# Folding the inverse transform over d a second time: odd and even frequencies apart, 144 columns to a product

## The chip, the cores and the metric

The kernel runs on one core of one Trainium2 chip. The metric is the device time of one execution in microseconds (us), as the median of several. Engines are named as in the profile: PE (TensorE, matrix products), PEld (its weight loads), DVE (VectorE), ACT (ScalarE), POOL (GpSimd) and SP (SyncE, which issues nearly all DMAs).

## The reference

The input x has 2048 rows (s) of 576 numbers (d). Rows are normalised, and two branches are added to x:

```python
xn = _layernorm(x, axis=-1)
# A: a filter in the frequencies of s and d
X = jnp.fft.rfft2(xn, axes=(-2, -1)) * (w_r + 1j * w_i)      # 2048 x 289
a = jnp.fft.irfft2(X, s=(S, D), axes=(-2, -1))
# B: a gated layer, F = 4608
h = _sigmoid(xn @ w_gate) * (xn @ w_up)
return x + a + h @ w_down
```

Everything is float32. The change concerns branch A alone, above all the last of its transforms, the inverse over d.

## The kernel before, in words

Products in float32 are made of two parts with a short mantissa (type fp32r, "hi" and "lo"): each factor is split, and three products (hi times hi, lo times hi, hi times lo) replace one. PE does all of it.

**Branch B** fills most of the span. `unit` (L667 on) makes one block of 128 of the 4608 hidden places for 1024 rows, with seven products (`prod`, L636) of seven instructions each, 512 columns wide, into PSUM banks A, B and E. The hidden values go through w_down in `down` (tile `po`, L743) and, in the second half of the rows, in `seven` (tile `ps`, L834), 288 columns wide. DVE adds `po` and `ps` into the accumulator `acc` or the sums `qs` (L747, L844).

**Branch A** is spread between these products in the second half of the program. Its steps are generators; the main loop calls `aside` after each of a unit's seven products, which moves each active generator to its next `yield`. A table (`begin`, from U1, U2, U3 at L41) says at which of these calls a step starts: `phase1b` (16 steps, forward over d and the first half of s), `phase2` (16 steps, second half of s, the filter, and the first half of the way back), `phase3` (16 steps t, a new one every 4.5 calls: second half of the way back over s, then the inverse over d). So the place of each instruction in PE's order is set by these numbers. DVE and ACT take theirs in nearly the program's order, moved a little by a scheduler.

The transform over d is **folded once**. With d measured from the middle, 287.5, cosines are even and sines are odd in d. So the cosine part is computed for 288 places only, the sine part too, and the two halves of d are their difference and sum. `COLS` orders the columns of x, w_down and the output so that the lower half stands first and the upper half, mirrored, behind it. The 289 frequencies stand in the order KOF (L44): 1 to 256, then 0, then 257 to 288, and one empty place make NQ = 290.

**A step of `phase3`** loads 2 x 128 rows of the intermediate result (`u`, from `sc2`), the matrices `ai` of that step and, for the first eight t, the rows of the result so far (`fin`, from `spill`); for the other eight, `acc` itself is added to. Then:

- `uh`, `ul` (L559, L560): the split of u. Products into `py` (L565), 290 columns: frequencies stand in the columns.
- `y` (L567): frequencies 1 to 256 are copied out of `py`. The remainder, FR = 33 columns, is split into `rp` (hi, lo, hi: 99 columns).
- `pz` (L577, L580): transposes, after which frequencies stand in the rows, 128 to a block k. z3h and z3l (L208, L209) are their two parts, z3r (L585, on ACT, the last of the three) is the remainder.
- `pe` (L594): for the cosine part e = 0 and the sine part e = 1 apart, 2 blocks x 3 products with z3h and z3l, then one with z3r. The constants `di` are the moving side, 288 columns; the z tiles are the weights. That is 14 products.
- the close: ACT copies the sine part to `od` (L596); DVE does lower - od, lower + cosine, upper + od, upper + cosine (L598, L599, L600, L601, each 288 wide). For the first eight t a DMA then writes the rows to the output.

`ps`, `po`, `py`, `pz`, `pe` and the like share one PSUM pool of two buffers (`pair`, tag `pp`), taken in turn: a tile can be filled when the tile two before it has been read. `stage3` (L622) makes room for phase 3 and loads `di`, and `stage2` clears the last column of zh and zl, which phase 2 doesn't write.

Of the kernel before, what the change touches and what calls it, by code (L numbers as in the profile page):

```python
# [24 lines left out]
FR = HD + 1 - 2 * P  # L25
# [18 lines left out]
KOF = np.array(list(range(1, 257)) + [0] + list(range(257, 289)))  # L44
# [19 lines left out]
def _constants():  # L64
# [5 lines left out]
    for e, v in ((0, np.cos(ang)), (1, -np.sin(ang))):  # L70
        m = np.zeros((HD, NQ))
        m[:, :KD] = v
        m[:, KD - 1 if e == 0 else KT * P] = 0.0
# [32 lines left out]

    a = np.where((KOF == 0) | (KOF == HD), 1.0, 2.0)[:, None] / (D * S)
    co, si = a * np.cos(ang.T), a * np.sin(ang.T)
    co[KD - 1] = 0.0
    si[KT * P] = 0.0  # L110
    t = np.zeros((P, 2, 5, HD), np.float32)
    for e, m in ((0, co), (1, si)):
        hi, lo = _split(m)
        for part, w in ((0, hi), (1, lo)):
            t[:, e, 2 * part] = w[:P]
            t[:, e, 2 * part + 1] = w[P:2 * P]
        t[:3 * FR, e, 4] = np.concatenate([hi[2 * P:], hi[2 * P:], lo[2 * P:]])
    out["di"] = t.reshape(P, 10 * HD)
# [4 lines left out]
COLS = np.concatenate([np.arange(HD), np.arange(HD, D)[::-1]])  # L123
# [3 lines left out]
def _layout(x, w_r, w_i, w_gate, w_up, w_down):  # L127

    ks = np.concatenate([np.arange(KT * P), np.tile(np.arange(KT * P, HD), 4)])
    w = np.stack([w_gate[COLS], w_up[COLS]]).reshape(2, 2, HD, NF, P)[:, :, ks]  # L130
    w = w[[1, 1, 0, 0], [0, 1, 1, 0]].reshape(4, KT + 1, P, NF, P).transpose(3, 2, 0, 1, 4)
    v = np.stack([w_r, w_i])[:, :, KOF].reshape(2, N1, N2 // 2, 2, KD).transpose(2, 1, 0, 3, 4)
    v = np.broadcast_to(v[:, None], (N2 // 2, 2, N1, 2, 2, KD))
    x = x.reshape(S, D)[ROWS][:, COLS]
    xt = x.reshape(NT, P, 2, HD)[..., ks].reshape(NT, P, 2, KT + 1, P).transpose(0, 4, 2, 3, 1)
    xg = xt[TPP:].reshape(2, TPC, P, 2, KT + 1, P).transpose(0, 3, 2, 4, 1, 5).reshape(2, 2, P, (KT + 1) * CW)
    lay = {"x": x.reshape(NT, P, D), "xt": xt.reshape(NT, P, 2 * (KT + 1) * P), "xg": xg, "ri": v.reshape(N2 // 2, P, 4 * KD),
           "w": w.reshape(NF, P, 4 * (KT + 1) * P), "wd": w_down[:, COLS].reshape(NF, P, D)}
    return {k: np.ascontiguousarray(a) for k, a in lay.items()}
# [9 lines left out]
def spectral_glu_kernel(ctx: ExitStack, tc: tile.TileContext, x, xt, xg, ri, w_in, w_down, out):  # L149
# [353 lines left out]
    def phase2(i):  # L503
# [4 lines left out]
        w = pool.tile([P, 2, 2, KD], F32, tag="ri", name=f"ri{i}", bufs=2)  # L508
# [14 lines left out]
        sw = pool.tile([P, 2, KD], F32, tag="sw", name=f"sw{i}")  # L523
        nc.scalar.activation(sw[:N1], pb[N1:, :, :KD], AF.Copy, scale=-1.0)
        nc.scalar.activation(sw[N1:], pb[:N1, :, :KD], AF.Copy)
        z = pool.tile([P, 2, KD], F32, tag="z", name=f"z{i}")
        t2 = pool.tile([P, 2, KD], F32, tag="t2", name=f"t2{i}")
        nc.vector.tensor_tensor(z, wr, pb[:, :, :KD], op=OP.mult)
# [3 lines left out]
        split(zh[:, :, :KD], zl[:, :, :KD], z)  # L532
# [10 lines left out]
    def phase3(t):  # L543
        pool, di = R["pool"], R["di"]
# [43 lines left out]
        for e in range(2):  # L588
            steps = []
            for k in range(2):  # L590
                steps += [(zh[:, k, e, :], di[:, e, k, :]), (zl[:, k, e, :], di[:, e, k, :]), (zh[:, k, e, :], di[:, e, 2 + k, :])]
            steps.append((zr[:3 * FR, e, :], di[:3 * FR, e, 4, :]))
            for n, (l, r) in enumerate(steps):
                nc.tensor.matmul(pe[:, e, :HD], l, r, start=n == 0, stop=n == len(steps) - 1)  # L594
        od = pool.tile([P, HD], F32, tag="od", name=f"od{t}")
        nc.scalar.activation(od, pe[:, 1, :HD], AF.Copy)  # L596
        lo, up = a[:, :HD], a[:, HD:]
        nc.vector.tensor_tensor(lo, lo, od, op=OP.subtract)  # L598
        nc.vector.tensor_tensor(lo, lo, pe[:, 0, :HD], op=OP.add)  # L599
        nc.vector.tensor_tensor(up, up, od, op=OP.add)  # L600
        nc.vector.tensor_tensor(up, up, pe[:, 0, :HD], op=OP.add)  # L601
# [9 lines left out]
    def stage2():  # L611
        pool = room("2")
        R["bm"] = bm = pool.tile([P, 4, P], F32R, name="bmt")
        load_r(bm, con["bm"].rearrange("p (k m) -> p k m", k=4))
        zh = pool.tile([P, 2, NQ], F32R, name="zh")
        zl = pool.tile([P, 2, NQ], F32R, name="zl")
        for z in (zh, zl):
            nc.vector.memset(f32(z)[:, :, KD:], 0.0)
# [606 lines left out]
```

## Time and profile before

| | |
|---|---|
| median of 3 runs | 1419.71 us (1419.65 to 1420.62) |
| the profiled execution | 1421.62 us |
| its span, first to last instruction | 1419.8 us |
| PE busy | 1405.9 us, 99% of the span, 7883 products |
| PEld busy | 1235.9 us, 87% |
| DVE busy | 1112.5 us, 78% |
| ACT busy | 640.6 us, 45% |
| DMA | 343.10 MB, mean 242 GB/s |
| mean granted PE clock | 0.997 |

The profile is of one execution. A group's row names line, engine, operation, the tiles (out<-in), shapes and count; then its busy time and the mean length of one; then the engine's idle time in front of it and what ended it. Products on PE overlap: one is as long as from its start to the end of its result, so that the distance between starts, in the timeline, is what a product costs in a stream. PEld rows are the weight loads, one to each product. Line numbers are those of the kernel before.

### The profile page before, as it was taken

The page shows a single profiled execution, that of the slowest core. Times are in us where ns is not written, and L with a number is a line of the kernel's source. Part 1 is how long each engine was busy: PE and PEld are TensorE (multiplying, and loading weights), DVE is VectorE, ACT ScalarE, POOL GpSimd, SP SyncE. Part 2 cuts the span into 40 slices and gives each one's busy share as a digit, 9 for nine tenths or more (in the row PEclk, how much of TensorE's full clock was granted, in tenths as well). Part 3 has the DMA queues.
Part 4 walks back from the last instruction along what each step waited for, and adds up shares of the span by engine and source line. Part 5 has one row for each costly group of instructions (what it writes and reads, how often), then busy time and mean ns, then how long its engine had stood idle before and what let it go on. Part 6 is the DMA issues. An engine that isn't in the chain of part 4 may idle for free. (4 is left out here: it accounts for less than half of the span.)

```text
span 1419.8 us, 20725 instructions
## 1 busy us (share of the span) xinstructions
PE 1405.9 (99%) x7883; PEld 1235.9 (87%) x7883; DVE 1112.5 (78%) x1722; ACT 640.6 (45%) x1035; POOL 3.3 (0%) x5
## 2 busy tenths in 40 slices
PE   8999999999999999999999999999999999999998
PEld 6888888888888888888888888888888889999897
DVE  6988888888888888789466888877878877766784
ACT  5644444444444443444235444434545534434431
POOL 0000000000000000000000000000000000000000
PEclk9999999999999999999999999999999999999999
DMA  6498677777777776675767777778888787766643
GB/s 250 181 329 308 256 267 262 270 263 270 263 269 263 269 263 247 242 254 176 270 217 234 224 234 223 217 245 267 275 269 272 236 290 221 247 215 204 195 126 84
DMA packets 130899, 343.10 MB, mean 242 GB/s; under 512 B 12176, under 2 KB 51632, under 8 KB 125936
## 3 DMA queue, kind: packets, MB, share of 16 engines
q1 hardware_dynamic: 129872, 340.47, 71.0%
q8 instruction: 62, 1.02, 0.3%
q10 hardware_dynamic: 928, 1.31, 0.3%
q14 instruction: 37, 0.30, 0.1%
HBM read 205.60 MB, written 136.13 MB: 241 GB/s over the span
## 5 line engine op out<-in xcount | busy, mean ns | idle before, releaser
L636 PE MATMUL pB<-X,w 128*128 128x512 f32 x1484 | 379.9, 393 | 0.0
L636 PEld LDWEIGHTS pB<-X,w 128*128 128x128 f32 x1484 | 268.0, 188 | 49.6 <-ACT v L700 1.3
L636 PE MATMUL pE<-X,w 128*128 128x512 f32 x1064 | 271.8, 392 | 0.5 <-DVE y L701 0.5
L636 PE MATMUL pA<-X,w 128*128 128x512 f32 x1008 | 261.4, 395 | 1.2 <-DVE X L445 0.8
L636 PEld LDWEIGHTS pE<-X,w 128*128 128x128 f32 x1064 | 193.2, 188 | 35.4 <-DVE y L701 1.0
L636 PEld LDWEIGHTS pA<-X,w 128*128 128x128 f32 x1008 | 184.5, 190 | 35.4 <-DVE X L445 1.7
L743 PE MATMUL po<-wd,hh 128*128 128x288 f32 x1216 | 210.8, 295 | 0.0
L834 PEld LDWEIGHTS ps<-wf,hs 128*128 128x128 f32 x1260 | 188.9, 188 | 17.9 <-ACT qs L842 0.9
L834 PE MATMUL ps<-wf,hs 128*128 128x288 f32 x1260 | 202.0, 295 | 0.4 <-ACT qs L842 0.4
L743 PEld LDWEIGHTS po<-wd,hh 128*128 128x128 f32 x1216 | 184.2, 188 | 11.8 <-ACT hh L726 0.4
L747 DVE TENSOR_TENSOR acc<-acc,po 128x576 f32<-128x576 f32 x168 | 125.7, 749 | 67.3 <-PE po L743 66.8
L240 ACT ACTIVATE w<-raw 128x768 fp32r<-128x768 f32 (+1 forms) x106 | 100.8, 952 | 93.1 <-PE pE L636 36.5
L743 PE MATMUL po<-wd,hl 128*128 128x288 f32 x608 | 128.7, 293 | 0.0
L844 DVE TENSOR_TENSOR qs<-qs,ps 128x576 f32<-128x576 f32 x112 | 84.1, 751 | 28.4 <-PE ps L834 27.4
L743 PEld LDWEIGHTS po<-wd,hl 128*128 128x128 f32 x608 | 98.7, 189 | 0.0
L701 DVE TENSOR_TENSOR y<-v,pE 128x512 f32<-128x512 f32 x68 | 46.7, 686 | 52.2 <-ACT v L700 51.3
L844 DVE TENSOR_TENSOR acc<-acc,ps 128x576 f32<-128x576 f32 x90 | 67.5, 750 | 23.3 <-PE ps L834 22.6
L242 DVE TENSOR_TENSOR w<-raw,w 128x512 fp32r<-128x512 f32 (+1 forms) x106 | 81.8, 772 | 3.2 <-ACT w L240 2.9
L721 DVE TENSOR_TENSOR y<-y,g 128x1024 f32<-128x1024 f32 x67 | 81.9, 1222 | 3.1
L770 ACT ACTIVATE hs<-y 128x512 fp32r<-128x512 f32 x105 | 64.8, 628 | 38.2 <-DVE y L721 14.6
L704 ACT ACTIVATE g<-pB 128x512 f32<-128x512 f32 x68 | 40.7, 598 | 89.9 <-PE pB L636 89.9
L700 ACT ACTIVATE v<-pB 128x512 f32<-128x512 f32 x68 | 40.6, 598 | 71.0 <-PE pB L636 70.7
(175 smaller groups left out, 1609.0 us busy)
## 6 DMA issues: line engine op xcount, KB each, us to landing
w<-wsp SPq DMA_DIRECT2D x246, 320.0 KB, 3.5
wsp<-w SPq DMA_DIRECT2D x34, 2240.0 KB, 7.8
raw<-in_w SPq DMA_DIRECT2D x34, 768.0 KB, 9.7
wdsp<-wd SPq DMA_DIRECT2D x36, 576.0 KB, 4.6
wf<-tsp SPq DMA_DIRECT2D x60, 288.0 KB, 3.9
wf<-wdsp SPq DMA_DIRECT2D x45, 288.0 KB, 3.9
std<-in_wd SPq DMA_DIRECT2D x36, 288.0 KB, 5.5
ri<-in_ri SPq DMA_DIRECT2D x16, 578.0 KB, 5.3
```

What stands on the lines that cost most here:

```text
L240: placed(nc.scalar.activation(o[:, :, :3, :], src, AF.Copy))
L242: placed(nc.vector.tensor_tensor(o[:, :, 3:, :], src[:, :, :KT, :], f32(o[:, :, :KT, :]), op=OP.subtract))
L636: nc.tensor.matmul(bank, w[:, sw, :], X[:, x, sx, :], start=start and j == 0, stop=stop and j == len(STEPS) - 1, skip_group_check=skip)
L700: nc.scalar.activation(v[:, 1], bank["B"], AF.Copy)
L701: nc.vector.tensor_tensor(y[:, 1], v[:, 1], bank["E"], op=OP.add)
L704: nc.scalar.activation(g[:, 1], bank["B"], AF.Sigmoid)
L721: nc.vector.tensor_tensor(y, y, g, op=OP.mult)
L743: nc.tensor.matmul(pd[:, b, :HD], h[i], w[k][b], start=g == 0 and n == 0, stop=g == G - 1 and n == 2)
L747: nc.vector.tensor_tensor(a, a, pd[:, :, :HD], op=OP.add)
L770: nc.scalar.activation(hs[:, 0], src, AF.Copy)
L834: nc.tensor.matmul(pd[:, i, :HD], h[:, a, m], w[:, b], start=q == 0, stop=q == 2)
L844: nc.vector.tensor_tensor(o, o, pd[:, :, :HD], op=OP.add)
```

## The change

The inverse over d is folded a second time. Within half of d, 288 places from the middle out, a cosine of an even frequency is even about the quarter, and that of an odd frequency odd; for sines it is the other way. So each part needs 144 places only (HQ), one set for odd and one for even frequencies, and the four quarters of d come from their sums and differences.

- KOF puts the 144 odd frequencies first, then an empty place (PAD), then the 145 even ones. Blocks for the transposes are places 0 to 127 (odd only) and 162 to 289 (even only); the remainder is the 34 places between them, 16 odd, the empty one and 17 even.
- `di` now has, for each part e, block k and half (hi, lo), 144 columns. The remainder's constants stand in `dr` (tile `drt`), still 288 wide, with zeros in the quarter set that a row has no part in. They are loaded separately.
- In `pe` the product with the remainder comes first and opens the PSUM bank; the twelve others add to one half of it, 144 columns each.
- The close: `ev` takes cosine part + od and cosine part - od (two operations of 288); one of 576 adds the even set of both to all four quarters (the same 288 numbers to both halves of the row); two of 288 add and subtract the odd set.
- `COLS` orders columns by quarters. `cf`, `ri` and the layouts of x, made on the host, follow the new orders; the remainder in `rp` has 3 x 34 = 102 columns. In phase 2 all 290 columns are worked on in place of 289, and the two memsets are gone.

```diff
-KOF = np.array(list(range(1, 257)) + [0] + list(range(257, 289)))
+KOF = np.array(list(range(1, HD, 2)) + [0] + list(range(0, HD + 1, 2)))
...
-COLS = np.concatenate([np.arange(HD), np.arange(HD, D)[::-1]])
+COLS = np.concatenate([HD - 1 - QTR, HD + QTR, QTR, D - 1 - QTR])
...
     def phase3(t):
...
-        nc.scalar.activation(y, py[:, :, :2 * P], AF.Copy)
+        main = py[:, :, :2 * (P + FR)].rearrange("p a (b n) -> p a b n", b=2)[..., :P]
+        nc.scalar.activation(y.rearrange("p a (b n) -> p a b n", b=2), main, AF.Copy)
         rp = pool.tile([P, 2, 3, FR], F32R, tag="rp3", name=f"rp3{t}")
-        rem = py[:, :, 2 * P:KD]
+        rem = py[:, :, P:P + FR]
...
         for e in range(2):
-            steps = []
+            nc.tensor.matmul(pe[:, e, :HD], zr[:3 * FR, e, :], dr[:3 * FR, e, :], start=True, stop=False, skip_group_check=True)
             for k in range(2):
-                steps += [(zh[:, k, e, :], di[:, e, k, :]), (zl[:, k, e, :], di[:, e, k, :]), (zh[:, k, e, :], di[:, e, 2 + k, :])]
-            steps.append((zr[:3 * FR, e, :], di[:3 * FR, e, 4, :]))
-            for n, (l, r) in enumerate(steps):
-                nc.tensor.matmul(pe[:, e, :HD], l, r, start=n == 0, stop=n == len(steps) - 1)
+                o = pe[:, e, (k + 1 + e) % 2 * HQ:((k + 1 + e) % 2 + 1) * HQ]
+                for n, (l, i) in enumerate(((zh, 0), (zl, 0), (zh, 1))):
+                    nc.tensor.matmul(o, l[:, k, e, :], di[:, e, k, i, :], start=False, stop=n == 2, skip_group_check=True)
         od = pool.tile([P, HD], F32, tag="od", name=f"od{t}")
         nc.scalar.activation(od, pe[:, 1, :HD], AF.Copy)
-        lo, up = a[:, :HD], a[:, HD:]
-        nc.vector.tensor_tensor(lo, lo, od, op=OP.subtract)
-        nc.vector.tensor_tensor(lo, lo, pe[:, 0, :HD], op=OP.add)
-        nc.vector.tensor_tensor(up, up, od, op=OP.add)
-        nc.vector.tensor_tensor(up, up, pe[:, 0, :HD], op=OP.add)
+        V = pool.tile([P, 2, 2, HQ], F32, tag="ev", name=f"ev{t}")
+        for i, op in ((0, OP.add), (1, OP.subtract)):
+            nc.vector.tensor_tensor(V[:, i].rearrange("p a q -> p (a q)"), pe[:, 0, :HD], od, op=op)
+        w = a.rearrange("p (s v q) -> p s v q", s=2, v=2)
+        nc.vector.tensor_tensor(w, w, V[:, :, 0].unsqueeze(1).to_broadcast([P, 2, 2, HQ]), op=OP.add)
+        for i, op in ((0, OP.add), (1, OP.subtract)):
+            nc.vector.tensor_tensor(w[:, i], w[:, i], V[:, :, 1], op=op)
...
     def stage3():
         pool = room("3")
-        R["di"] = di = pool.tile([P, 2, 5, HD], F32R, name="dit")
-        load_r(di, con["di"].rearrange("p (e k n) -> p e k n", e=2, k=5))
+        R["di"] = di = pool.tile([P, 2, 2, 2, HQ], F32R, name="dit")
+        R["dr"] = dr = pool.tile([P, 2, HD], F32R, name="drt")
+        load_r(di, con["di"][:, :8 * HQ].rearrange("p (e k i q) -> p e k i q", e=2, k=2, i=2))
+        load_r(dr, con["di"][:, 8 * HQ:].rearrange("p (e n) -> p e n", e=2))
```

PE's order stays the same but for the products of `pe` themselves. Here is the first step of phase 3 on PE before, from the products of a unit in front of `pe` to those behind it (128x288 is the result, rows by columns; dit is `di`):

```order
L834 MATMUL ps_5_1_11030<-wf_5_10891,hs_5_10941 128x288 x6
L594 MATMUL pe_11040<-dit,z3h_11015 128x288
L594 MATMUL pe_11040<-dit,z3l_11016 128x288
L594 MATMUL pe_11040<-dit,z3h_11015 128x288 x2
L594 MATMUL pe_11040<-dit,z3l_11016 128x288
L594 MATMUL pe_11040<-dit,z3h_11015 128x288
L594 MATMUL pe_11040<-dit,z3r_11017 128x288
```

The same place now, the first seven of its 14 products:

```order
L846 MATMUL ps_5_1_11030<-wf_5_10891,hs_5_10941 128x288 x6
L600 MATMUL pe_11040<-drt,z3r_11017 128x288
L604 MATMUL pe_11040<-dit,z3h_11015 128x144
L604 MATMUL pe_11040<-dit,z3l_11016 128x144
L604 MATMUL pe_11040<-dit,z3h_11015 128x144 x2
L604 MATMUL pe_11040<-dit,z3l_11016 128x144
L604 MATMUL pe_11040<-dit,z3h_11015 128x144
```

Seven instructions stay seven, with seven weight loads; six have half the columns, and the one with z3r has moved to the front.

On DVE, the close of the first step before, with the operations around it:

```order
L701 TENSOR_TENSOR y_10900<-v_10899,pE_10903 128x512
L844 TENSOR_TENSOR qs<-qs,ps_5_1_11030 128x576
L598 TENSOR_TENSOR fin_10875<-fin_10875,od_11055 128x288
L600 TENSOR_TENSOR fin_10875<-fin_10875,od_11055 128x288
L599 TENSOR_TENSOR fin_10875<-fin_10875,pe_11040 128x288
L601 TENSOR_TENSOR fin_10875<-fin_10875,pe_11040 128x288
L844 TENSOR_TENSOR acc<-acc,ps_6_0_11070 128x2x288
```

And now:

```order
L713 TENSOR_TENSOR y_10900<-v_10899,pE_10903 128x512
L856 TENSOR_TENSOR qs<-qs,ps_5_1_11030 128x576
L609 TENSOR_TENSOR ev_11057<-pe_11040,od_11055 128x288 x2
L611 TENSOR_TENSOR fin_10875<-fin_10875,ev_11057 128x576
L613 TENSOR_TENSOR fin_10875<-fin_10875,ev_11057 128x288 x2
L856 TENSOR_TENSOR acc<-acc,ps_6_0_11072 128x2x288
```

Four operations have become five, the one of 576 between the pairs; only the first two read `pe`.

More of the change, by code (lines that the diff above doesn't have):

```diff
@@ L70, in _constants @@
     for e, v in ((0, np.cos(ang)), (1, -np.sin(ang))):
-        m = np.zeros((HD, NQ))
-        m[:, :KD] = v
-        m[:, KD - 1 if e == 0 else KT * P] = 0.0
+        m = np.where(FREQ, v, 0.0)
         hi, lo = _split(m)
@@ L104, in _constants @@
     out["bm"] = b.reshape(P, 4 * P)
[L107 to L112, printed above, removed]
-        hi, lo = _split(m)
[L114 to L118, printed above, removed]
+    a = np.where((KOF == 0) | (KOF == HD), 1.0, 2.0)[:, None] / (D * S) * FREQ[:, None]
+    ang = 2 * np.pi * KOF[:, None] * (QTR[None, :] + 0.5) / D
+    t = np.zeros((P, 2, 2, 2, HQ), np.float32)
+    r = np.zeros((P, 2, HD), np.float32)
+    for e, m in ((0, a * np.cos(ang)), (1, a * np.sin(ang))):
+        m[KOF == (HD, 0)[e]] = 0.0
+        hi, lo = _split(m)
+        for k, rows in enumerate((slice(0, P), slice(NQ - P, NQ))):
+            t[:, e, k, 0], t[:, e, k, 1] = hi[rows], lo[rows]
+        h, l = np.zeros((2, FR, HD), np.float32)
+        for s, v in ((h, hi), (l, lo)):
+            v = v[P:NQ - P]
+            o = ODD[P:NQ - P]
+            s[o, (1 - e) * HQ:(2 - e) * HQ] = v[o]
+            s[~o, e * HQ:(e + 1) * HQ] = v[~o]
+        r[:3 * FR, e] = np.concatenate([h, h, l])
+    out["di"] = np.concatenate([t.reshape(P, 8 * HQ), r.reshape(P, 2 * HD)], 1)
     out["id"] = np.eye(P, dtype=np.float32)
     return out
-COLS = np.concatenate([np.arange(HD), np.arange(HD, D)[::-1]])
+COLS = np.concatenate([HD - 1 - QTR, HD + QTR, QTR, D - 1 - QTR])
 ROWS = np.arange(S).reshape(N1, N2).T.ravel()
@@ L507, in phase2 @@
         nc.sync.dma_start(x2, sc1.rearrange("(p kl) n -> p kl n", kl=N2)[:, kl:kl + 2])
-        w = pool.tile([P, 2, 2, KD], F32, tag="ri", name=f"ri{i}", bufs=2)
+        w = pool.tile([P, 2, 2, NQ], F32, tag="ri", name=f"ri{i}", bufs=2)
         nc.sync.dma_start(w.rearrange("p a j n -> p (a j n)"), ri[i])
@@ L522, in phase2 @@
                 nc.tensor.matmul(pb[:, j, :NQ], bm[:, k, :], m[:, j, :], start=n == 0, stop=n == 2)
[L523 to L528, printed above, removed]
+        sw = pool.tile([P, 2, NQ], F32, tag="sw", name=f"sw{i}")
+        nc.scalar.activation(sw[:N1], pb[N1:, :, :NQ], AF.Copy, scale=-1.0)
+        nc.scalar.activation(sw[N1:], pb[:N1, :, :NQ], AF.Copy)
+        z = pool.tile([P, 2, NQ], F32, tag="z", name=f"z{i}")
+        t2 = pool.tile([P, 2, NQ], F32, tag="t2", name=f"t2{i}")
+        nc.vector.tensor_tensor(z, wr, pb[:, :, :NQ], op=OP.mult)
         nc.vector.tensor_tensor(t2, wi, sw, op=OP.mult)
@@ L543, in phase3 @@
     def phase3(t):
-        pool, di = R["pool"], R["di"]
+        pool, di, dr = R["pool"], R["di"], R["dr"]
         u = pool.tile([P, 2, NQ], F32, tag="u3", name=f"u3{t}", bufs=2)
```

23 lines of the change are left out of this document (14 added, 9 removed).

## The prediction

> **What bounds the kernel now.** I read the page first, then the busy time by stretches, the waits, and last the timeline around one step of the changed phase. On the page PE is busy for nearly the whole span:
>
> ```profile
> span 1419.8 us, 20725 instructions
> PE 1405.9 (99%) x7883; PEld 1235.9 (87%) x7883; DVE 1112.5 (78%) x1722; ACT 640.6 (45%) x1035; POOL 3.3 (0%) x5
> ```
>
> The changed phase, `phase3`, runs from about 1150 to 1394 us. Two stretches of the view by windows cover it (columns: window, its length, busy us and instructions of PE, PEld, DVE, ACT, POOL, granted clock, DMA share, GB/s):
>
> ```profile
> 1180.00:1300.00 120.00, 120.00 (x716) 108.39 (x715) 87.77 (x146) 51.43 (x108) 0.00 (x0) 1.00 0.72 227
> 1300.00:1420.00 120.00, 115.09 (x701) 104.29 (x699) 79.52 (x123) 39.76 (x82) 0.00 (x0) 1.00 0.48 140
> ```
>
> PE has no gap in the first and 4.9 us in the second, which also holds the tail; DVE is busy for 73% and 66%. The waits say the same from both sides (engine and line, what it waited for, total us, times, longest):
>
> ```profile
> PE pE L636 <- DVE y L701: 0.5, 1, 0.5
> PE ps L834 <- ACT qs L842: 0.4, 1, 0.4
> PE po L743 <- DVE acc L747: 0.3, 1, 0.3
> DVE acc L747 <- PE po L743: 66.8, 52, 5.4
> DVE qs L844 <- PE ps L834: 27.4, 36, 1.8
> DVE acc L844 <- PE ps L834: 22.6, 28, 2.1
> ```
>
> PE waits for DVE for tenths of a microsecond in the whole span; DVE waits for PE for over 100 us in these three rows alone. So here the end moves by what PE's own stream of products gains or loses, and other engines' work counts only once it makes PE wait.
>
> **What one step of `phase3` costs on PE.** The products of tile `pe`, by kind, with their counts over the 16 steps:
>
> ```profile
> L594 PE MATMUL pe<-dit,z3h x128: 292/296/403, 1174.3 to 1391.7; 128*128 128x288 f32 x128
> L594 PE MATMUL pe<-dit,z3l x64: 290/296/298, 1174.5 to 1391.6; 128*128 128x288 f32 x64
> L594 PE MATMUL pe<-dit,z3r x32: 297/298/302, 1175.1 to 1391.9; 99*128 99x288 f32 x32
> ```
>
> That is 14 a step. The 296 ns are start to end of one; products overlap, so what counts is the distance from start to start. The timeline of the first step gives it (start, length, engine, line):
>
> ```profile
> 1174.35 0.29 PE L594 MATMUL pe<-dit,z3h 128*128 128x288 f32 x1
> ...
> 1176.21 1.79 PE L636 MATMUL pB<-X,w 128*128 128x512 f32 x7
> ...
> 1177.83 0.96 PE L834 MATMUL ps<-wf,hs 128*128 128x288 f32 x6
> ```
>
> Fourteen products in 1176.21 - 1174.35 = 1.86 us: **132.9 ns** each with 288 columns. Seven with 512 columns in 1.62 us: 231.4 ns. So a column costs (231.4 - 132.9) / 224 = 0.44 ns and a product 6 ns besides.
>
> **The change, part by part.** It leaves 14 products a step: the two remainder products (z3r) keep 288 columns, the other 12 go to 144. That is 192 in all (128 + 64). If columns alone set the distance, 144 of them would take 6.3 + 144 x 0.44 = 69.6 ns. But the number of weight loads stays, one of 128 columns for each product, and a load has a floor of its own. No product in the kernel with full 4-byte weights and so few columns shows it directly; it shows where PE stood idle and two loads followed with nothing in front (PEld rows, two places):
>
> ```profile
> 1316.72 0.19 PEld L594 LDWEIGHTS pe<-dit,z3h 128*128 128x128 f32 x1 [0.33 <-ACT z3r L585]
> 1316.83 0.19 PEld L594 LDWEIGHTS pe<-dit,z3l 128*128 128x128 f32 x1
> ```
>
> ```profile
> 964.69 0.19 PEld L538 LDWEIGHTS pc<-zh,bmt 128*128 128x128 f32 x1 [0.20 <-ACT zh L208]
> 964.80 1.02 PEld L636 LDWEIGHTS pA<-X,w 128*128 128x128 f32 x5
> ```
>
> Both pairs are 0.11 us apart, though one load lasts 0.19. The transposes, with 128 columns on both sides, give the same in a stream:
>
> ```profile
> L577 PE MATMUL pz<-idf,y x64: 270/272/328, 1171.3 to 1386.6; 128*128 128x128 f32 x64
> ```
>
> ```profile
> 1386.29 0.60 PE L577 MATMUL pz<-idf,y 128*128 128x128 f32 x4
> ...
> 1386.65 0.39 PE L580 MATMUL pz<-idr,rp 128*99 128x128 f32 x2
> ...
> 1386.87 1.83 PE L636 MATMUL pE<-X,w 128*128 128x512 f32 x7
> ```
>
> Four in 0.60 us, the last 0.272 long: (0.60 - 0.272) / 3 = 109.3 ns, where their columns alone would need 6.3 + 56 = 63 ns. I take **109.3 ns** for a product of 144 columns: the columns fit under the load. The bounds are 69.6 ns (loads hidden after all) and 132.9 ns (no gain).
>
> The Trainium skill has a rule for each side. "TensorE: Matmul & The Clock Gate", section "LDWEIGHTS (loading the stationary operand)", gives the load as the weight's columns over 1.2, in ns: 107 for 128, with which the sum would be 192 x 26 = 5.0 us; the 0.11 us between loads agree. The same page's section "Back-to-back issue gap" gives about 81 ns per product in a stream of loads and products with 128 columns, and 131 with 512; between the two, 144 columns would come to some 83 ns, an estimate, and the sum to 9.6 us. The 231 ns measured here for 512 columns contradict it, and no run here shows it for a short product.
>
> The sum: 192 x (132.9 - 109.3) ns = **4.5 us less on PE**, 0.28 us in each of 16 steps, all of it on the path.
>
> *VectorE.* The four closing operations become five. One step as it is, with what follows:
>
> ```profile
> 1176.85 0.46 DVE L598 TENSOR_TENSOR fin<-fin,od 128x288 f32<-128x288 f32 x1 [1.12 <-ACT od L596]
> 1177.23 0.45 DVE L600 TENSOR_TENSOR fin<-fin,od 128x288 f32<-128x288 f32 x1
> 1177.60 0.44 DVE L599 TENSOR_TENSOR fin<-fin,pe 128x288 f32<-128x288 f32 x1
> 1177.96 0.45 DVE L601 TENSOR_TENSOR fin<-fin,pe 128x288 f32<-128x288 f32 x1
> ...
> 1178.83 0.75 DVE L844 TENSOR_TENSOR acc<-acc,ps 128x576 f32<-128x576 f32 x1 [0.42 <-PE ps L834]
> ...
> 1180.23 0.96 PE L834 MATMUL ps<-wf,hs 128*128 128x288 f32 x6
> ...
> 1181.02 0.29 PE L565 MATMUL py<-uh,ai 128*128 128x290 f32 x1
> ```
>
> ```profile
> L560 DVE TENSOR_TENSOR ul<-u,uh 128x580 fp32r<-128x580 f32 x16 | 12.1, 758 | 2.2 <-ACT uh L559 1.8 <-DMA w<-wsp 0.3
> ```
>
> Four operations of 288 stay, 0.37 us apart; one of 576 comes, near the 0.76 us of the row of 580. So DVE works 0.76 us longer a step, 12 us in all, in about 240 us with some 70 us of idle time in the two stretches above. What is queued behind it is the add of the next `ps`, and PE waits for that add only for its buffer. There are two buffers in the pool of `pe`, `ps`, `py`, `pz`, taken in turn. After L601 DVE stood idle for 0.42 us, so the add would end 0.34 us later, at 1179.9; its buffer is taken by `py` at 1181.02, 1.1 us on. The buffer of `pe` is taken at 1180.23, and its last reader is now the second operation, not the fourth: 0.74 us sooner. I cost this at nothing; without that cover it is up to 12 us.
>
> *The remainder product goes first,* and reads z3r, the last tile made. The row of 1316.72 shows that the first product of `pe` waited for z3r already: `pe` takes the buffer that z3r is read from. Nothing new to wait for: nothing.
>
> *Constants and stage 2.* `dit` shrinks from 1.47 to 0.88 MB and comes in two loads, one more on SP's queue behind which the weights `w` stand. These wait for PE themselves:
>
> ```profile
> SPq L287 <- PE pB L636: 154.6, 89, 4.7
> ```
>
> One issue takes about 0.4 us there, in a queue that stands still for PE: nothing, or 0.4 us once. `ri` grows by 0.3%, operations of 578 become 580, and two memsets of a few columns go. All off PE's path: nothing. A few DVE operations swap places in stage 2 and 3, which may move PE's short waits by some tenths either way.
>
> **Against which time.** The profiled execution took 1421.62 us, its span 1419.80; the change makes them about 1417.1 and 1415.3. The median of the runs is 1419.71, 1.9 below the profiled one; the same 4.5 us off it give **1415.2 us**.
>
> **The rivals.**
> *A (forecast): the load is the floor,* 109 ns, 1415.2 us. For it: both pairs of loads and the transposes. Chance 0.72.
> *B: loads overlap more deeply,* and products come at between 70 and 100 ns. At 70 the gain is 192 x 63.3 = 12.2 us, 1407.5 us. For it speaks only that PEld rows last 0.19 us yet overlap; against it, the 0.11 us. The page's back-to-back figure lies inside it. Chance 0.07.
> *C: short products in this 4-byte type pass their columns more than once.* Narrower than 288 the trace has none but the transposes, and the two of L580 at 0.22 / 2 = 0.11 us each speak against it only if a transpose runs as an ordinary product does. The place is the 192 products; the turning point is 132.9 ns. Two passes give 6.3 + 127 = 133 ns, no change, 1419.7 us (chance 0.04). Four give 259.5 ns: 192 x 126.6 = 24.3 us more, **1444.0 us**, slower (chance 0.08).
> *D: DVE becomes late.* If all of its 12 us reach PE, 1419.7 - 4.5 + 12.1 = 1427.3 us. It decides from where the added 0.76 us a step exceed the slack, which is 0.42 us of idle time and then 1.1 us up to `py`. Against it: that slack, and the idle time. Chance 0.04; that part of it eats the gain down to under 2.8 us, 0.05.
>
> **How the numbers follow.** A measurement of this kernel can tell about 0.2%, 2.8 us, from no change. Faster by more: A and B less a little of A that ends just short, 0.76. Within: two passes, part of D and that remainder, 0.12. Slower: four passes and all of D, 0.12. The range takes in both bounds of the unknown distance, 1407 (69.6 ns) to 1420 (132.9 ns), and leaves out 0.12.
>
> **What would show it.** Right: the distance between the products of `pe` is 0.109 us, a step takes 2 x 0.133 + 12 x 0.109 = 1.57 us in place of 1.86, PEld rows of `pe` stand 0.11 us apart, and PE's idle time in phase 3 is as before. A step of 1.1 us shows B, of 1.86 or 3.4 us C. D would show as PE rows waiting for `acc`, `qs` or `y` on DVE, and as more PE idle time. It is wrong if the step's 14 products don't come closer together, or if the 0.28 us a step are given back at the next buffer.

## The result, and the profile after

| | before | changed |
|---|---|---|
| median | 1419.94 us (21 runs, 1419.20 to 1421.65) | 1417.93 us (21 runs, 1417.26 to 1419.47) |
| ratio, 95% interval | | 0.9986 (0.9980 to 0.9992) |
| profiled execution: span | 1419.8 us | 1415.8 us |
| from the first product of `pe` to the last of `po` | 240.8 us | 238.7 us |

The change saves 2.0 us, 0.14%. The forecast was 4.5.

The span isn't the number to read. The two executions differ by 2.0 us when phase 3 begins; in the thirteen profiles of this study phase 3 begins anywhere from 1172.1 to 1174.7 us, with the wide products and with the narrow ones alike. The difference is made at the very start: the 401st product of PE starts at 83.3 to 86.1 us, and from there to the first product of `pe` all thirteen profiles take 1088.6 to 1089.0 us. It goes with the granted clock of the first 60 us, here before and then changed (view by windows, columns as in the prediction; the clock is the third figure from the end):

```profile
0.00:60.00 60.00, 52.88 (x254) 41.02 (x255) 46.51 (x122) 37.97 (x80) 3.29 (x5) 0.94 0.53 196
```

```profile
0.00:60.00 60.00, 52.15 (x262) 40.09 (x263) 48.17 (x125) 39.68 (x83) 3.29 (x5) 1.00 0.56 204
```

The seven profiles in which phase 3 begins later than 1173 us are the seven with a mean clock of 0.997 over the span. The medians show it too: over the comparison sets of the experiments the kernel before took 1421.09 us at 0.997 (median of 31 runs) and 1419.85 at 0.998 (31). So the mechanism is read from phase 3, from the start of the first product of `pe` to that of the last of `po`, and the verdict from the ratios. That stretch went from 240.8 to 238.7 us, 2.1 less. For the changed kernel its ends stand in these two rows (line, engine, operation, count: shortest/median/longest ns, first to last start):

```profile
L600 PE MATMUL pe<-drt,z3r x32: 292/339/403, 1172.3 to 1387.0; 102*128 102x288 f32 x32
L755 PE MATMUL po<-wb,hp x192: 289/295/398, 1361.1 to 1411.0; 128*128 128x288 f32 x192
```

The 14 products of the first step in the timeline of the changed kernel (start, length, engine, line):

```profile
1172.31 0.30 PE L600 MATMUL pe<-drt,z3r 102*128 102x288 f32 x1
1172.45 0.23 PE L604 MATMUL pe<-dit,z3h 128*128 128x144 f32 x1
1172.52 0.27 PE L604 MATMUL pe<-dit,z3l 128*128 128x144 f32 x1
1172.63 0.39 PE L604 MATMUL pe<-dit,z3h 128*128 128x144 f32 x2
1172.85 0.28 PE L604 MATMUL pe<-dit,z3l 128*128 128x144 f32 x1
...
1173.88 1.83 PE L648 MATMUL pB<-X,w 128*128 128x512 f32 x7
```

A step takes 1173.88 - 1172.31 = 1.57 us where it took 1.86. The distance is 0.11 us between the short products, except from the first one behind a product of 288 columns to the next, where a load has already gone ahead (1172.45 to 1172.52, 0.07 us, which is what the prediction worked out for the columns alone). The loads stand as far apart as the products:

```profile
1172.45 0.19 PEld L604 LDWEIGHTS pe<-dit,z3l 128*128 128x128 f32 x1
1172.56 0.30 PEld L604 LDWEIGHTS pe<-dit,z3h 128*128 128x128 f32 x2
```

So the gain came as worked out, 0.29 us in this step, and part of it went elsewhere. The waits of PE from 1150 us on name where. Before there was one, `po` behind DVE at the very end; now:

```profile
PE pB L648 <- ACT pB L699: 0.5, 1, 0.5
PE py L575 <- DVE acc L856: 0.4, 1, 0.4
PE po L755 <- DVE acc L759: 0.3, 1, 0.3
PE py L575 <- issue: 0.2, 1, 0.2
```

Laying the starts of the products of both traces side by side (their order on PE differs only within `pe` and in stage 6, where one product of `pE` has moved ahead of five of `py`, at no cost) gives four places at which the distance to the next product has grown. Stage t reaches from the `pe` of step t, counted from 0, to that of the next step. The places are stage 4, where `py` starts 0.53 us later than it could (1234.87); stage 7, `ps` 0.11 us (1274.93); stage 10, `py` 0.41 us (1319.64); stage 13, `pB` 0.62 us (1359.37). Behind each stall the second product stands 0.08 to 0.11 us further off as well. In sum 2.0 us.

The place in stage 4, on DVE and on PE. Before:

```profile
1232.30 1.28 DVE L771 TENSOR_TENSOR hs<-y,hs 128x512 fp32r<-128x512 f32 x2
1233.61 0.46 DVE L598 TENSOR_TENSOR fin<-fin,od 128x288 f32<-128x288 f32 x1
...
1235.08 0.68 DVE L808 TENSOR_TENSOR y<-y,y 128x512 f32<-128x512 f32 x1
1235.68 0.75 DVE L844 TENSOR_TENSOR acc<-acc,ps 128x576 f32<-128x576 f32 x1
...
1237.78 0.29 PE L565 MATMUL py<-uh,ai 128*128 128x290 f32 x1
```

Changed:

```profile
1229.16 1.28 DVE L783 TENSOR_TENSOR hs<-y,hs 128x512 fp32r<-128x512 f32 x2
1230.36 1.41 DVE L820 TENSOR_TENSOR y<-y,y 128x512 f32<-128x512 f32 x2
1231.69 0.81 DVE L609 TENSOR_TENSOR ev<-pe,od 128x288 f32<-128x288 f32 x2
1232.53 0.76 DVE L611 TENSOR_TENSOR fin<-fin,ev 128x576 f32<-128x576 f32 x1
1233.33 0.83 DVE L613 TENSOR_TENSOR fin<-fin,ev 128x288 f32<-128x288 f32 x2
1234.07 1.41 DVE L856 TENSOR_TENSOR acc<-acc,ps 128x576 f32<-128x576 f32 x2
```

```profile
1233.55 0.96 PE L846 MATMUL ps<-wf,hs 128*128 128x288 f32 x6
1234.87 0.40 PE L575 MATMUL py<-uh,ai 128*128 128x290 f32 x1 [0.36 <-DVE acc L856]
```

`py` takes the buffer that the first of the two adds to `acc` reads. Before, that add ended at 1236.43 and `py` came at 1237.78: 1.35 us of slack. Measured from the start of the two `hs`, the add begins 3.38 us later before and 4.91 now. The close is 0.91 us longer (1233.61 to 1235.08, now 1231.69 to 1234.07), and **two operations `y` have moved ahead of it** (sums of hidden values, from which the factor `hs` of a later product `ps` is made), of which one stood ahead of the add already: some 0.6 us more. And PE could be at `py` 5.18 us after that start (six `ps` take 0.79 us) in place of 5.48, which is the step's own gain. 1.35 - 1.53 - 0.30 = -0.48 us, against 0.53 that `py` lost. None of the three alone is enough. By the same sum the close and the order together would exceed the slack by 0.2 us, and either one together with the earlier PE would not (the runs below with the old close, and those with the order held, have no wait here).

In stages 7 and 10 `y` operations have moved ahead of the close too, and in stage 13 two more copies on ACT ahead of the one that PE waits for. Before, and now:

```profile
1360.97 0.63 ACT L770 ACTIVATE hp<-y 128x512 fp32r<-128x512 f32 x1 [0.40 <-DVE y L721]
1361.79 0.58 ACT L687 ACTIVATE pB<-pA 128x512 f32<-128x512 f32 x1 [0.18 <-PE pA L636]
1362.28 1.14 ACT L770 ACTIVATE hp<-y 128x512 fp32r<-128x512 f32 x2
```

```profile
1357.68 1.14 ACT L782 ACTIVATE hp<-y 128x512 fp32r<-128x512 f32 x2
1358.73 0.59 ACT L699 ACTIVATE pB<-pA 128x512 f32<-128x512 f32 x1
```

### The profile page after: what moved, and what is told of

The parts are those of the page before. It is cut to its first block, busy times and chain, and to the rows that moved or that the text cites. A ratio compares the mean times of both kernels' runs of the same rounds, so it can differ in the third digit from the quotient of the medians.

```text
span 1415.8 us, 20731 instructions
## 1 busy us (share of the span) xinstructions
PE 1400.5 (99%) x7883; PEld 1228.9 (87%) x7883; DVE 1123.7 (79%) x1736; ACT 640.3 (45%) x1035; POOL 3.3 (0%) x5
```

## The experiments

Four theories were set against each other. **L**: the close, longer by one DVE operation, makes PE wait. **O**: the order does it; with shorter products the scheduler, which works from its own estimates, puts other DVE and ACT work ahead of the close. **P**: the earlier PE runs into work that ends when it did before, whatever the order. **E**: something else, away from these places. All results (ratio to the kernel before, run beside it; "phase 3" is the stretch defined above in the one profile of each kernel, 240.8 us before):

| run | products, close, order | median us | ratio (95%) | phase 3 |
|---|---|---|---|---|
| changed | 144, new, by the scheduler | 1417.93 | 0.9986 (0.9980 to 0.9992) | 238.7 |
| e1_old_close | 144, old, by the scheduler | 1417.88 | 0.9983 (0.9974 to 0.9992) | 238.9 |
| e2_wide | 288, new, by the scheduler | 1420.74 | 1.0001 (0.9993 to 1.0010) | 240.6 |
| e3_pool | 144, new with one operation on POOL | 1421.41 | 1.0002 (0.9994 to 1.0011) | 240.9 |
| e4_pin | 144, new, ACT's copies kept in order | 1417.86 | 0.9981 (0.9972 to 0.9990) | 238.2 |
| e5_old_held | 144, old, close ahead of `y` | 1416.84 | 0.9979 (0.9970 to 0.9988) | 237.3 |
| e6_held_last | 144, new, close ahead of `y` | 1417.33 | 0.9980 (0.9971 to 0.9989) | 237.4 |
| e7_held_first | 144, new, its first half ahead of `y` | 1417.34 | 0.9978 (0.9969 to 0.9987) | 237.1 |
| e8_72 | 72, new, by the scheduler | 1415.39 (one run) | | 236.7 |
| e9_wide_late | 288, new, `y` ahead of the close | 1421.11 | 1.0003 (0.9994 to 1.0012) | 240.6 |
| e10_one_held | 144, new, close ahead of one `y` | 1416.82 | 0.9976 (0.9967 to 0.9985) | 237.3 |
| e11_wide_exact | 288, new, stage 4 as in the changed | 1419.98 | 1.0001 (0.9992 to 1.0010) | 240.5 |

**The old close.** Four DVE operations again, with the products of the change; the sums of the odd and even parts over the quarters are left out of the computation.

```diff
-        for i, op in ((0, OP.add), (1, OP.subtract)):
-            nc.vector.tensor_tensor(V[:, i].rearrange("p a q -> p (a q)"), pe[:, 0, :HD], od, op=op)
...
+        nc.vector.tensor_tensor(lo, lo, od, op=OP.subtract)
+        nc.vector.tensor_tensor(lo, lo, pe[:, 0, :HD], op=OP.add)
+        nc.vector.tensor_tensor(up, up, od, op=OP.add)
+        nc.vector.tensor_tensor(up, up, pe[:, 0, :HD], op=OP.add)
```

> The changed kernel with the close of the kernel before: four operations of 288 on DVE, no operation of 576. It leaves out the sums over the odd and even sets, so the columns of branch A are wrong; PE's products are those of the change. In the changed kernel's trace PE waits at four places of phase 3 which were free before, about 2.2 us: three of them behind DVE (near 1234, 1275 and 1319 us), one behind ACT (1358.5 us), where ACT now copies two hp tiles ahead of pB<-pA. Theory L (DVE's longer close makes PE late): the three places behind DVE go, the one on ACT stays, since ACT's order there is still the changed one: 1419.9 - 4.6 + 0.7 = 1416.0 us, ratio to before 0.997. Rival O (only the new order on ACT and DVE costs, not the added operation): mostly as the changed kernel, 1417 to 1418 us, ratio 0.9986. Rival P (narrow products cost PE something later, whatever DVE does): 1417.9 us, with the waits in other places.

1417.88 us: nothing was won by the shorter close, and L as a single cause falls. The wait of stage 4 is gone, though both `y` still stand ahead of the close there, as the sum above would have it (0.91 us of it was the close), but those of stages 10 and 13 stand, and that of stage 7 has grown. The timeline of this kernel there, DVE and PE:

```profile
1274.17 0.69 DVE L818 TENSOR_TENSOR y<-y,y 128x512 f32<-128x512 f32 x1
1274.78 0.45 DVE L608 TENSOR_TENSOR fin<-fin,od 128x288 f32<-128x288 f32 x1
...
1275.88 0.45 DVE L611 TENSOR_TENSOR fin<-fin,pe 128x288 f32<-128x288 f32 x1
```

```profile
1276.43 1.06 PE L844 MATMUL ps<-wf,hs 128*128 128x288 f32 x6 [0.68 <-ACT v L704]
```

The row names ACT, but the product starts 0.10 us after the fourth operation of the close has ended, which is the last to read `pe` and frees the buffer. With the new close only the first two read `pe`, and the wait is 0.11 us. So the new close wins 0.7 us here, about the 0.6 that it costs in stage 4.

**Products of 288 columns with zeros**, the new close.

```diff
-    t = np.zeros((P, 2, 2, 2, HQ), np.float32)
+    t = np.zeros((P, 2, 2, 2, HD), np.float32)
...
-                o = pe[:, e, (k + 1 + e) % 2 * HQ:((k + 1 + e) % 2 + 1) * HQ]
+                o = pe[:, e, :HD]
```

> The changed kernel, but each of the twelve products of pe has 288 columns again, with zeros in the quarter set that it has no part in: PE's cost of before, DVE's close of the change. The result is the reference's. ACT's order at t = 13 is that of before here. Theory L: PE gives DVE 0.29 us more a step, so that the waits behind DVE are fewer than in the changed kernel but some are left: 0.5 to 1.5 us over before, 1420.4 to 1421.4 us, ratio 1.0004 to 1.001. Rival O: with other orders on DVE and ACT, 1420 to 1421 us. Rival P: 1419.9 us, no waits that before doesn't have. Rival E (something else in the change, say the constants or stage 2, gives or costs): clearly off this, under 1419 or over 1422 us.

1420.74 us, no change, and phase 3 within 0.2 us of before with none of the four waits. The longer close, the new constants, the new order of columns and the remainder product in front cost nothing that phase 3 shows; the forecast's zeros hold, as long as the products stay wide.

**The operation of 576 on POOL.**

```diff
-        nc.vector.tensor_tensor(w, w, V[:, :, 0].unsqueeze(1).to_broadcast([P, 2, 2, HQ]), op=OP.add)
...
+        nc.gpsimd.tensor_tensor(w, w, V[:, :, 0].unsqueeze(1).to_broadcast([P, 2, 2, HQ]), op=OP.add)
```

> The changed kernel with the operation of 576 moved from DVE to POOL, as the last of the close; DVE keeps four operations of 288, as before. The result is the reference's. Theory L: as e1_old_close, 1416.0 us, ratio 0.997, if POOL's own operation is in nobody's way (nothing but the output of the step waits for it). Rival O: 1417 to 1418 us. If POOL slows DVE or takes so long that the rows of the next step wait, over 1418 us; its row shows how long it takes.

1421.41 us; the whole gain is gone. The operation takes POOL 1.41 to 1.45 us in fifteen steps and 1.83 in one, where DVE takes 0.76. DVE's own work beside it can slow down; `ul`, 0.76 us otherwise, took 0.90, 1.33 and 2.01 us in three steps. The longest of each:

```profile
1360.74 1.83 POOL L613 TENSOR_TENSOR acc<-acc,ev 128x576 f32<-128x576 f32 x1 [13.88 <-DVE acc L612]
```

```profile
1361.18 2.01 DVE L570 TENSOR_TENSOR ul<-u,uh 128x580 fp32r<-128x580 f32 x1
```

**ACT's copies kept in the order in which they are written.**

```diff
-        nc.scalar.activation(hs[:, 0], src, AF.Copy)
+        copy = nc.scalar.activation(hs[:, 0], src, AF.Copy)
+        if len(key) == 2 and key[0] >= NF:
+            tc.keep_in_program_order(copy)
```

> The changed kernel with ACT's copies into hp held at their place in the program's order, so that at t = 13 ACT makes pB<-pA ahead of the two hp copies, as in the kernel before. Nothing else is changed; the result is the reference's. If PE's wait of 0.7 us at 1358.5 us comes from ACT's order: that wait goes, 1417.9 - 0.7 = 1417.2 us, ratio 0.9981, and the three places behind DVE stay. If it comes from DVE's longer close (DVE frees late what hp needs): no change, 1417.9 us.

The wait of `pB` in stage 13 is gone, the three on DVE stand, and phase 3 is 0.5 us shorter than in the changed kernel (0.62 and 0.11 won, 0.27 lost at `py`, 1363.42, whose `ul` DVE now makes behind the close and three operations `hp` and ends at 1363.36). In the median that can't be told apart.

**Order held: the old close again, the new close, and its first half.** In stages 4, 7 and 10 the factor's `y` may not run ahead of the close; ACT's copies as in the run before. In the first of the three, the sums over the quarters are left out once more. The second is the changed kernel with

```diff
+    def behind(ins):
+        if "close" in R:
+            tc.add_manual_dep(ins.ins, R["close"].ins.name, ...)
...
+        if t in (4, 7, 10):
+            R["close"] = R["at"]
+        else:
+            R.pop("close", None)
...
-            nc.vector.tensor_tensor(A[put], A[a], A[b], op=op)
+            behind(nc.vector.tensor_tensor(A[put], A[a], A[b], op=op))
```

where `R["at"]` is the last operation of the close, and in the third kernel the second one.

> The first run's kernel (144-place products, the close of before, so the sums of the odd and even products are left out) with three kinds of DVE operation held behind the close in stages 4, 7 and 10, namely the factor's y, and with ScalarE's hp copies of the last stages kept in the order in which they are written. Theory O (the 2.6 us come back because shorter products let the scheduler put other DVE and ScalarE work ahead of the close): the waits near 1234, 1275, 1319 and 1358 us are gone, and the time comes to between 4.0 and 4.7 us below the kernel before, ratio about 0.9969. Theory P (the products' gain makes TensorE run into work that ends when it did before, in whatever order): waits of the same sum appear at the same or neighbouring products, and the time stays about 2.5 us below, ratio about 0.9983.

> The changed kernel whole, with the factor's y held behind the last of the close's five operations in stages 4, 7 and 10, and the hp copies kept in written order. Theory O: at least 1.5 of the 2.6 us are won, 3.6 to 4.6 us below the kernel before (ratio 0.9968 to 0.9975), with the three waits gone. Theory P: 2 to 3 us below, ratio about 0.9983, the waits in other places. A third outcome: y, now later, is what the products of the next block wait for, which shows as py waiting for DVE L820 and costs 0.3 to 1 us at each of the three stages.

> As the run before, but the factor's y is held only behind the two operations of the close that read PSUM, so that the three that follow can lie behind it. Theory O: the same gain as with all five ahead at 1275 us (there it is the product's buffer that is late, which these two free), and less at 1234 and 1319 us, where the sums behind the close are late: 3 to 4.3 us below the kernel before, ratio about 0.9974. Theory P: ratio about 0.9983.

All four waits are gone in all three; the lists of waits of the second and third name only `po` at the very end, as before the change. Phase 3 takes 237.1 to 237.4 us, 3.4 to 3.7 below before, against 2.1 in the changed kernel. The first of them and the run with the old close have the same products and the same close: 237.3 against 238.9 us comes from the order, which was changed on DVE and ACT, and on PE at two places (stages 11 and 13), by the scheduler. P, by which the waits would have moved elsewhere, falls in the main: what comes new is a delay at `py` of stage 13, again behind `ul`, of 0.6 us in the first kernel and 0.3 in the other two. O holds, with less than it hoped for (3.5 rather than 4.0 to 4.7). In the medians the step over the changed kernel is 0.6 to 1.1 us, within their intervals: 17 of the 32 runs of these kernels had a granted clock of 0.997, and 2 of the 26 of the kernel before beside them.

**72 columns.** The other half of each z product's columns is left out of the computation.

```diff
-                    nc.tensor.matmul(o, l[:, k, e, :], di[:, e, k, i, :], ...)
+                    nc.tensor.matmul(o[:, :HQ // 2], l[:, k, e, :], di[:, e, k, i, :HQ // 2], ...)
```

> The changed kernel with the 192 folded products cut from 144 columns to 72 (the other half of each z is left out of the computation; everything else as in the changed kernel). If the distance between two such products is set by the load of the weights, it stays within 2 ns of the 110 ns that they stand apart now, and each step of 14 at 1.57 us; if by 0.44 ns a column and 46 ns, it falls to about 78 ns and a step to about 1.1 us.

```profile
1172.15 0.30 PE L600 MATMUL pe<-drt,z3r 102*128 102x288 f32 x1
1172.28 0.20 PE L604 MATMUL pe<-dit,z3h 128*128 128x72 f32 x1
1172.32 0.27 PE L604 MATMUL pe<-dit,z3l 128*128 128x72 f32 x1
1172.43 0.39 PE L604 MATMUL pe<-dit,z3h 128*128 128x72 f32 x2
1172.65 0.28 PE L604 MATMUL pe<-dit,z3l 128*128 128x72 f32 x1
...
1173.68 0.70 PE L648 MATMUL pB<-X,w 128*128 128x512 f32 x2
```

The distance is 0.11 us with half the columns, so the columns don't set it. Nor is it a least time from product to product: from the first short product behind one of 288 columns to the next, where the load has gone ahead, it is 0.04 us (1172.28 to 1172.32) in place of 0.07, for which the prediction's 6.3 ns and 0.44 ns a column would give 38 ns in place of 70. That leaves the load of the weights. The step is 1.53 us for it, not 1.57. That gain is only lent: the first product of `pB` then stands 0.075 us further from the second than before the change, where it is 0.038 with 144 columns.

Yet phase 3 is 2.1 us shorter than in the changed kernel, with none of the four waits. The scheduler, with other lengths to go by, has put the close ahead again. This kernel's DVE in stage 4:

```profile
1229.08 1.29 DVE L783 TENSOR_TENSOR hs<-y,hs 128x512 fp32r<-128x512 f32 x2
1230.28 0.82 DVE L609 TENSOR_TENSOR ev<-pe,od 128x288 f32<-128x288 f32 x2
1231.01 0.68 DVE L820 TENSOR_TENSOR y<-y,y 128x512 f32<-128x512 f32 x1
1231.61 0.75 DVE L611 TENSOR_TENSOR fin<-fin,ev 128x576 f32<-128x576 f32 x1
1232.28 0.75 DVE L856 TENSOR_TENSOR acc<-acc,ps 128x576 f32<-128x576 f32 x1
```

Counted from the two `hs`, the add starts 1.71 us sooner than in the changed kernel (3.20 against 4.91), and `py` starts without a wait, at 1234.31. Nobody held anything here.

**The order of the changed kernel, with wide products.** The second run's kernel, with the close of the three stages held behind the same `y`; in a second kernel two adds are held as well, so that stage 4 has the changed kernel's order on DVE operation by operation.

```diff
+            if i == 0 and t in (4, 7, 10):
+                R["first"], R["held"] = ev, (t, {4: 4, 7: 3, 10: 3}[t])
...
-            nc.vector.tensor_tensor(A[put], A[a], A[b], op=op)
+            behind(nc.vector.tensor_tensor(A[put], A[a], A[b], op=op))
```

Here `behind` lets the first operation of the close depend on the n-th `y` written behind it.

> The second run's kernel (products 288 columns wide with zeros in the half that isn't wanted, the close of five operations) with the close of stages 4, 7 and 10 held behind the factor's y operations that stand ahead of it in the changed kernel. The products cost what they did before the change, so TensorE is nowhere earlier. Theory O (the order alone makes the waits): waits of 0.3 to 0.5 us at py of stages 4 and 10 and at ps of stage 7, in sum 0.8 to 1.3 us over the second run's kernel, ratio to the kernel before 1.0006 to 1.001 where that had 1.0001. Theory P (only earlier products run into a wait): none of the three waits, ratio as in the second run. Both together: the waits appear, each smaller by the 0.3 us that the products of its stage gained.

> The ninth run's kernel with two sums held as well, so that the order of VectorE in stage 4 is that of the changed kernel operation by operation (the first sum of the next product behind all five operations of the close), and in stage 10 all but one. In the changed kernel the product py of stage 4 starts 0.53 us later than in the kernel before, and that of stage 10 0.41 us. Theory O (the order alone makes the wait): py of stage 4 waits as long here, 0.4 to 0.6 us. Theory P (the wait comes of the earlier TensorE alone): no wait. Both: 0.2 to 0.3 us at stage 4, since the narrow products bring TensorE 0.3 us nearer to it within a stage, and 0.1 or nothing at stage 10. In the median this is at most 1 us, ratio 1.0003 to 1.0010.

None of the four waits is there in either, and phase 3 is as with wide products before. But that the order alone costs nothing isn't shown by it. In stage 10 of the second, `py` comes 0.45 us behind the end of the addition that frees its buffer (1320.74 and 1321.19); yet one `hs`, some 0.6 us, doesn't stand ahead of the close as it does in the changed kernel. In stage 4 of the first kernel the add to `acc` still stood ahead of three of the close's operations. In the second the order of stage 4 is the changed one, and DVE runs it in the same time; but the scheduler answered by putting two products of `pB` between `ps` and `py`:

```profile
1235.09 0.96 PE L859 MATMUL ps<-wf,hs 128*128 128x288 f32 x6
1235.88 0.62 PE L661 MATMUL pB<-X,w 128*128 128x512 f32 x2
1236.35 0.30 PE L585 MATMUL py<-uh,ai 128*128 128x290 f32 x1
```

```profile
1230.42 1.29 DVE L796 TENSOR_TENSOR hs<-y,hs 128x512 fp32r<-128x512 f32 x2
...
1235.34 1.50 DVE L869 TENSOR_TENSOR acc<-acc,ps 128x576 f32<-128x576 f32 x2
```

The first add ends near 1236.1, so `py` in its old place, 1235.88, would have waited some 0.2 us, an estimate, and what the sum above gives for the close and the order together. It isn't shown, since the two products cover it.

**One `y` held in each stage.** The changed kernel with the least that restores the order, and ACT's copies in place.

```diff
+        if t in (4, 7, 10):
+            R["close"], R["held"] = R["at"], {4: 3, 7: 2, 10: 3}[t]
```

`R["held"]` counts the `y` operations; the one that brings it to zero is put behind the close's second operation.

> The changed kernel whole, with a single y operation held behind the first two operations of the close in each of stages 4, 7 and 10, and the hp copies kept in written order; this is nearly the order that the kernel with 72 columns got by itself. Theory O: the waits near 1234, 1275, 1319 and 1358 us are gone, phase 3 loses 1.3 us or less beside its products' gain, and the time comes to 3.4 to 4.2 us below the kernel before (ratio 0.997 to 0.9976). Theory P: ratio about 0.9984, as the changed kernel.

1416.82 us, ratio 0.9976, at the edge of what was expected; phase 3 is 3.5 us shorter than before. All four waits of the changed kernel are gone. Two smaller ones are new. In stage 7 `py` starts 0.25 us late and its second product another 0.11, behind an add to `acc` that ends at 1278.89:

```profile
1278.15 0.74 DVE L866 TENSOR_TENSOR acc<-acc,ps 128x576 f32<-128x576 f32 x1
...
1278.94 0.40 PE L581 MATMUL py<-uh,ai 128*128 128x290 f32 x1
```

In stage 13 the second product of `py` is 0.19 us late and the third another 0.10, behind `ul`, which ends at 1362.46:

```profile
1361.70 0.76 DVE L576 TENSOR_TENSOR ul<-u,uh 128x580 fp32r<-128x580 f32 x1
...
1362.51 0.40 PE L581 MATMUL py<-ul,ai 128*128 128x290 f32 x1
```

PE's order in phase 3 is that of the changed kernel, product by product, in this run and in the one that held only ACT's copies. So the comparison is of the order on DVE and ACT alone: against that run, 238.2 us, three DVE operations put back are worth 0.9 us, and the copies were worth 0.5. At a granted clock of 0.997 the medians were 1417.92 us (5 runs) for this kernel, 1419.01 (5) for the changed one and 1421.09 (31) for the one before. By its median it is the fastest version that computes the whole result, though its interval overlaps that of the changed kernel, and by phase 3 the version with the close's first half ahead is 0.2 us shorter.

## Why the prediction was right and wrong

- **PE is the bound, and its stream sets the time.** Right, and the account of phase 3 closes by the starts of the products: 4.3 us gained inside the 14 products, 0.2 lost next to them, 2.0 lost at the four places, 2.1 left.
- **109.3 ns per product of 144 columns, 1.57 us a step, 4.5 us in sum.** Right in mechanism and size: 0.11 us and 1.57 us were measured, and with 72 columns it is still 0.11. The distances inside the 14 fell by 4.3 us in all 16 steps together. B and C are out. The Trainium skill, "TensorE: Matmul & The Clock Gate", section "LDWEIGHTS (loading the stationary operand)", gives the load as the columns of the weights over 1.2, in ns, which is 107 for 128, and the 0.11 us agree. The 81 ns per product of 128 columns in the Trainium skill, same title, section "Back-to-back issue gap", are not reached here in a stream of 144 columns nor of 72.
- **The products next to the 14.** Not in the sum: the one behind them, whose weights now come later, pays 0.04 us a step, 0.6 us; the distance from the last of `pe` to it falls by 0.02, 0.4 us. The net 0.2 leaves about 4.1 us.
- **The close at nothing.** Its cover, 1.1 us at the first `py`, is there in the first step, and with wide products it holds at all four places. The close itself came out 0.92 us longer where its operations follow one another, not 0.76. This step failed in its reach: the slack was read in one step and taken for all, and it was read for the order of before. In stage 4 the same slack of 1.35 us was used up by three things at once, the close (0.91), the order (0.6) and the earlier PE (0.3).
- **"A few DVE operations swap places in stage 2 and 3, which may move PE's short waits by some tenths either way."** This is the term that was too small: not some tenths but 2.0 us at four places, three behind DVE and one behind ACT, whose order was not looked at. That is most of the 2.4 us by which the stretch missed 4.5; the other 0.4 are the 0.2 by which the 14 products gained less and the 0.2 next to them. Putting the order back won 0.9 us on DVE and 0.5 on ACT; the rest, 0.65, is the two new delays of the last run, behind the add to `acc` in stage 7 and `ul` in stage 13.
- **D, rival,** was put as DVE alone, with a chance of 0.05 for a part that eats the gain to below 2.8 us. That is the outcome, 2.0, but by another way: DVE's added time alone does nothing (wide products), and PE's speed alone little (order held). The two meet where the scheduler has queued other work ahead. By the signs that the prediction named, the distances came as for A, but "PE's idle time in phase 3 is as before" did not, and at a next buffer a part of the gain was given back.
- The predicted 1415.2 us lies 2.7 below the measured 1417.93, which is inside the range; the change is within 0.2% and not beyond it, which had been given 0.12. The range reached down to no change at all, so that the time lies in it says little for the mechanism; the distances do.
- Also open: a change of the order with wide products and PE's order kept could not be had, since the scheduler moved products itself; and why the granted clock of the first 60 us differs from execution to execution, with which the beginning of phase 3 moves by up to 2.6 us.

## What to carry to other kernels

Where a scheduler orders instructions by its own estimates, a change of their lengths is also a change of order, on engines that the edit doesn't touch; so compare the order of every engine at each repetition, and take the slack at the tightest one, not at the first. A buffer's release has its cover used up by the sum of what is queued ahead, what was added, and what the waiting engine has gained; check the three together. A product that is already shorter than the load of its weights gains nothing more by having fewer columns: here 144 and 72 both stand 0.11 us apart.

## What the runs showed of the hardware

- A product of 72 columns stands as far from the next as one of 144, 0.11 us. Only the first short one behind a product of 288 columns is followed sooner, after 0.07 us (144 columns) or 0.04 us (72); and behind the 14, the second product of 512 columns comes 0.038 us (144) or 0.075 us (72) later than before the change.
- After a stall of PE, the second product stands another 0.08 to 0.11 us further off, so that a wait costs more than its row says: in stage 4 the row says 0.36 us, and PE lost 0.53 and 0.11.
- An addition of 128x576 took POOL 1.41 to 1.45 us in fifteen steps and 1.83 in one, where DVE takes 0.76; `ul`, which DVE does in 0.76 us, took up to 2.01 beside it, and 0.92 in the mean of its 16 (0.76 in the changed kernel).
- The mean granted clock of the first 60 us was 0.94 in one execution and 1.00 in another, and the 401st product started at 85.3 and 83.5 us; from there on the two took the same time up to phase 3, within 0.2 us.
